# A gated mix of segment attention and a spectral filter on one core: the numerators of a segment loaded and normalised in two pieces instead of five, with rows dealt to chunks in another order and a new instruction plan

## The chip, the core and the metric

The kernel runs on one core of a Trainium2 chip. The metric is the device time of one execution in microseconds (us). Before the change the median of three runs is 243.28 us (242.96 to 243.37). The text calls the engines as the profile does: PE (TensorE's matmuls), PEld (its weight loads), DVE (VectorE), ACT (ScalarE), POOL (GpSimd) and SP (SyncE, which here only issues DMAs).

## The reference

Two branches read the same x of 2048 tokens by 640 features and are mixed token by token:

```python
g = sigmoid((x * gate_w).sum(-1, keepdims=True))
a = A(x)                       # 32 heads of 20, 4 segments of 512 tokens
b = irfft2(rfft2(x) * (w_r + 1j * w_i))
return g * a + (1 - g) * b

def A(x):                      # per head and segment s
    p = softmax(q @ k.T * scale + causal_mask)
    a_dot = p @ v
    a_mem = (phi(q) @ M) / (phi(q) @ z + 1e-6)     # memory of the earlier segments
    o = sigmoid(beta) * a_mem + (1 - sigmoid(beta)) * a_dot
    M, z = M + phi(k).T @ v, z + phi(k).sum(rows)
    return o @ wo              # o: the heads side by side, 640 columns
```

So 640 rows (32 heads times 20 elements) of attention output, each 512 tokens long per segment, must be divided by their head's denominator, joined by the memory's answer, and contracted with the 640 rows of wo.

## The kernel before

**The two branches.** The attention branch goes through the segments one by one: `project` makes q, k and v on PE, `qk_unit` makes the logits (in row tiles, four heads at once) with one exponential on ACT per unit and causal masks on DVE or POOL (`mask`, L1254 and L1255), `pv` multiplies by v. `mem_read_tile` asks the memory: matmuls into PSUM, then on DVE a sum (L1056), a reciprocal (L1059) and the product `mem_mul` (L1061 for segments 1 and 2, L1072 for segment 3), which writes the SBUF tile `mem`. The spectral branch (`fft`) is cut into small matmuls that fill PE between the attention units: for each of 16 frequency groups two products with the filter (`W_mul`, L1346, DVE) and two combinations (`W_add`, L1351, DVE or POOL). Its last step, `sum_Db` (L1388, DVE), makes the table `G`.

**Numerators.** `pv` leaves 512 tokens by 32 rows per head in PSUM (20 numerators, the denominator, padding); they are copied (`ub`) and stored in a DRAM scratch `u_scr`, head after head. When a segment's denominators have been inverted (`denominators`, a table `r4` with one row per head), `finish_tile` for its first quarter (a = 0) loads the 640 numerator rows back as the tile `oU`: a partition per head and part (32 heads times 4 = 128 partitions), five chunks of 512 tokens. Chunk c holds the elements 4c to 4c+3 of every head. One DMA (`ld_u`, L1412) and one multiplication by `r4` (`normal`, L1414, DVE or POOL) are made for each chunk. Segment 3 does the same for 24 heads with 5 parts and 4 chunks; its last 8 heads go another way. `mem_mul` writes its product in the same order of rows, so that after a store to `o_scr` and a transposing load (`mT`) it can be added to `oU` (`addmem`, L1427). Chunk c is then the stationary operand of the c-th `oproj` matmul of every output tile; `late_weights` loads the rows of wo in the order of the chunks (`wo` and, for segment 3, `wo3`).

**The order of the work.** Nothing is scheduled on the chip. `record` lists 2243 operations with what they read and write; `PLAN` is a list of as many integers, in the order in which the operations are emitted. The quotient by 16 is the operation's number, `v // 2 % 8` its engine and `v % 2` chooses a form for those matmuls that have two (`mode=-1`): whole array (one instruction of 128 columns of weights, L401) or four column tiles of 32 (L399). A second list gives each PSUM buffer its bank. `Sched.emit` puts the waits on semaphores. Every engine runs its own operations in that order, and one that waits holds up all behind it; SP issues nearly all DMAs in that order too. So PE's stream is a sequence of matmuls of three shapes: whole array, column tiles (`pv`, half of `v`, `Fb` always; others by choice) and row tiles (the logits, shown as 20*64 and 20*128).

Of the kernel before, what the change touches and what calls it, by code (L numbers as in the profile page):

```python
# [8 lines left out]
ALU = mybir.AluOpType  # L9
# [3 lines left out]
P = 128  # L13
S = 2048
D = 640
H = 32
DH = 20
NSEG = 4
L = 512
KD = 321  # L20
VW = 22
# [303 lines left out]
def dap(ap, off, *dims):  # L325
    return bass.AP(tensor=ap.tensor, offset=ap.offset + off, ap=[list(q) for q in dims])
# [24 lines left out]
class Kern:  # L351
# [65 lines left out]
    def dma(self, dst, src, nbytes, r, w, tr=False, name="", after=(), queues=("sp",)):  # L417
# [350 lines left out]
    def late_weights(self):  # L768
        b = self.b
# [722 lines left out]
```

## Time and profile before

| | |
|---|---|
| median of three runs | 243.28 us |
| the profiled execution: its time / its span | 241.93 us / 240.2 us |
| granted TensorE clock in it | 0.999 |
| largest group of instructions: ACT's exponentials, L1229 | 64 x 1878 ns = 120.2 us |
| DMA: moved, packets | 43.92 MB, 61897 |
| DMA issues of `oU<-u_scr` | 19 (15 of 128 KB, 4 of 120 KB) |

The span goes from the first instruction to the last; 1.7 us of the execution's time lie outside it. The page gives for each engine the time in which it ran an instruction, a row of 40 digits (tenths of each fortieth of the span), and the chain of work that ended last: from the last instruction back, at each step to what released it. Groups are shown as "out<-in" by the program's names with the count, the total and the mean in ns, and the idle time of the engine just before them. A window row gives the busy time of every engine in one stretch.

### The profile page before, as it was taken

The numbers are of one execution on the slowest core, as the hardware profiler recorded it, in microseconds if no ns is written. First come the engines' busy times: TensorE is split into PE (matmuls) and PEld (weight loads), VectorE is DVE, ScalarE is ACT, GpSimd is POOL, SyncE is SP. The second block draws the span as 40 slices with busy tenths as digits, with TensorE's granted clock in tenths as the row PEclk, the third lists the DMA queues.
The fourth block names the chain that finished last, engine by engine and source line by source line (L and its number), as shares of the span: only waits on it lengthen the run. The fifth ranks groups of instructions, "written<-read, shape, count | busy, mean of one in ns | idle before, by whom it ended". The sixth has DMA issues, their size and how long they took to land.

```text
span 240.2 us, 9491 instructions
## 1 busy us (share of the span) xinstructions
PE 220.6 (92%) x4004; PEld 138.0 (57%) x4018; DVE 209.2 (87%) x476; ACT 198.7 (83%) x226; POOL 134.2 (56%) x205
## 2 busy tenths in 40 slices
PE   6989979999999889999998999999978999799994
PEld 2865546665654547555755457656544555466673
DVE  0889979999999899999999989899999996867752
ACT  2489879999999988988999799997989598589321
POOL 8613154547647594676659563694686606753100
PEclk9999999999999999999999999999999999999999
DMA  7999979989959764269769847565875899594323
GB/s 196 317 242 271 235 221 154 296 217 166 233 153 206 177 179 142 68 185 176 236 183 200 182 113 232 167 184 178 200 174 167 177 214 120 114 191 129 109 104 113
DMA packets 61897, 43.92 MB, mean 183 GB/s; under 512 B 31232, under 2 KB 58656, under 8 KB 61856
## 3 DMA queue, kind: packets, MB, share of 16 engines
q1 hardware_dynamic: 60816, 42.76, 76.0%
q8 instruction: 31, 0.51, 0.9%
q10 hardware_dynamic: 1040, 0.57, 0.8%
q14 instruction: 10, 0.08, 0.1%
HBM read 23.42 MB, written 13.87 MB: 155 GB/s over the span
## 4 chain that ended last, share of the span: by engine, by line
PE 43%; DVE 32%; ACT 8%; POOL 6%; issue 5%; DMA 3%; SPq 2%; DVEq 0%; POOLq 0%
PE psum L401 39%; ACT ex L1229 5%; POOL exc L1255 4%; DVE Pt L1346 4%; PE psum L399 4%; DVE G L1388 3%; DVE ub L408 2%; DVE Yt L1351 2%; DMA x<-in_A_x_dram 2%; DVE va L408 2%; SPq L423 2%; DVE Ac L408 2%; DVE mem L1072 2%; ACT exc L1225 2%; DVE Bt L408 1%
## 5 line engine op out<-in xcount | busy, mean ns | idle before, releaser
L1229 ACT ACTIVATE ex<-psum 128x2048 bf16<-128x2048 f32 x64 | 120.2, 1878 | 12.8 <-PE psum L401 12.1
L1255 POOL TENSOR_SCALAR_AFFINE_SELECT ex<-ex 128x256 bf16<-128x256 bf16 (+2 forms) x93 | 54.5, 593 | 49.7 <-ACT ex L1229 34.9
L1255 POOL TENSOR_SCALAR_AFFINE_SELECT exc<-exc 128x512 bf16<-128x512 bf16 (+3 forms) x23 | 29.1, 1271 | 10.4 <-DVE exc L1254 7.3
L401 PE MATMUL psum<-qkp 20*64 20x64 bf16 (+5 forms) x1024 | 31.1, 266 | 3.4 <-DMA qkp<-qk_scr 1.3
L401 PE MATMUL psum<-xT,wk 128*128 128x256 bf16 (+1 forms) x276 | 29.7, 273 | 0.5 <-issue 0.5
L401 PE MATMUL psum<-xT,wq 128*32 128x256 bf16 (+1 forms) x161 | 25.1, 326 | 1.2 <-issue 1.0
L1346 DVE TENSOR_TENSOR Pt<-psum,Wt 128x642 bf16<-128x642 f32 x32 | 25.7, 821 | 0.3 <-PE psum L401 0.2
L401 PE MATMUL psum<-wv,xT 128*32 128x320 bf16 (+3 forms) x387 | 24.5, 300 | 0.4 <-DVE Pt L1346 0.4
L401 PEld LDWEIGHTS psum<-qkp 20*64 20x64 bf16 (+1 forms) x1024 | 12.6, 100 | 19.1 <-ACT ex L1229 8.6
L401 PEld LDWEIGHTS psum<-xT,wk 128*128 128x128 bf16 (+1 forms) x276 | 19.9, 97 | 5.2 <-issue 2.0
L401 PE MATMUL psum<-ex,va 128*32 128x384 bf16 (+2 forms) x384 | 20.4, 320 | 1.9 <-POOL ex L1255 0.7
L401 PE MATMUL psum<-wo,oU 128*128 128x320 bf16 (+1 forms) x114 | 18.6, 300 | 0.0
L836 POOL TENSOR_TENSOR xsb<-xf 128x320 bf16<-128x320 bf16 (+2 forms) x12 | 9.0, 750 | 16.7 <-DVE xsb L836 13.7
L401 PEld LDWEIGHTS psum<-wv,xT 128*32 128x32 bf16 (+1 forms) x387 | 13.8, 96 | 6.4 <-issue 1.1
L408 DVE CAST ub<-psum 128x512 bf16<-128x512 f32 x23 | 15.7, 683 | 1.9 <-PE psum L401 1.4
L408 ACT ACTIVATE ot<-psum 128x320 bf16<-128x320 f32 x21 | 8.7, 440 | 10.5 <-PE psum L399 4.2
L1225 ACT ACTIVATE exc<-psum 128x1024 bf16<-128x1024 f32 (+1 forms) x12 | 15.7, 1308 | 1.8 <-PE psum L401 1.4
L1388 DVE TENSOR_TENSOR G<-eo,psum 128x320 bf16<-128x320 f32 x32 | 14.9, 481 | 1.8 <-ACT eo L408 1.4
L401 PE MATMUL psum<-big,Ac 128*128 128x161 bf16 (+2 forms) x93 | 14.2, 258 | 0.7 <-DVE mem L1061 0.3
L1254 DVE TENSOR_TENSOR ex<-ex,mk 128x256 bf16<-128x256 bf16 (+2 forms) x35 | 13.7, 397 | 1.0 <-ACT ex L1229 0.9
L401 PEld LDWEIGHTS psum<-xT,wq 128*128 128x128 bf16 (+1 forms) x175 | 10.4, 97 | 7.2 <-issue 0.7
L401 PEld LDWEIGHTS psum<-ex,va 128*32 128x32 bf16 x384 | 8.0, 95 | 11.2 <-issue 2.7
(145 smaller groups left out, 459.5 us busy)
## 6 DMA issues: line engine op xcount, KB each, us to landing
qkp<-qk_scr SPq DMA_DIRECT2D x28, 160.0 KB
tt<-tab_tt SPq DMA_DIRECT2D x8, 512.0 KB, 4.2
u_scr<-ub SPq DMA_DIRECT2D x15, 256.0 KB, 3.9
qk_scr<-qu SPq DMA_DIRECT2D x12, 256.0 KB, 2.1
xsb<-in_A_x_dram SPq DMA_DIRECT2D x8, 320.0 KB, 4.9
oU<-u_scr SPq DMA_DIRECT2D x15, 128.0 KB, 2.6
out_dram<-ot SPq DMA_DIRECT2D x12, 160.0 KB
Wt<-in_B_w_r_dram SPq DMA_DIRECT2D x16, 80.2 KB, 4.1
```

The costliest lines, as they stand in the source:

```text
L399: h = e.matmul(dst, wt, r_, start=st, stop=sp_, **{**kw, "tile_position": (0, q), "skip_group_check": True})
L401: h = e.matmul(o_, l_, r_, start=st, stop=sp_, **({**kw, "skip_group_check": True} if mode < 0 else kw))
L408: fns = {"act": lambda e: e.activation(dst(), src(), ACT.Copy), "dve": lambda e: e.tensor_copy(dst(), src())}
L423: return e.dma_start(d_, s_)
L836: self.either(lambda e, dst=dst, src=src, d0=d0, n=n, op=op: e.tensor_tensor(xs.ap(o + dst, [D, 2], [1, n]), xf.ap(src + d0, [321, 2], [1, ...
L1072: self.one("dve", lambda e, q0=q0, n=n, d0=d0, dst=dst, src=src, bc=bc: e.tensor_tensor(self.mem.ap(o + d0, *dst), self.ps(bank, q0 * VW, ...
L1225: self.one("act", lambda e, i=i: e.activation(self.exc.ap(self.exco(s, g + i), [192, 4], [768, m], [1, 128]), self.ps(bank, 128 * i, [512, ...
L1229: self.one("act", lambda e: e.activation(self.ex.ap(*d), self.ps(bank, *q), ACT.Exp, scale=SC), n, [bank], [self.exb(s, 2 * pr + gp, ks + ...
L1254: fns = {"dve": lambda e: e.tensor_tensor(av(d0), av(s0), mk(), ALU.min), "pool": lambda e: e.affine_select(ap(d0), ap(s0), [[0, 4 * m], [ ...
L1255: "pool": lambda e: e.affine_select(ap(d0), ap(s0), [[0, 4 * m], [step, n // 64], [1, 64]], ALU.is_ge, 0.0, base=base, channel_multiplier=-1)}
L1346: self.one("dve", lambda e, ri=ri, Pt=Pt, Wt=Wt, wo_=wo_, bank=bank: e.tensor_tensor(Pt.ap(ri * 322, [644, 2], [1, KD]), self.ps(bank, 0, ...
L1388: self.one("dve", lambda e, q=q, n2=n2, bank=bank, eo=eo: e.tensor_tensor(self.G.ap(n2 * D + 639 * q, [1 - 2 * q, 320]), eo.ap(q, [1, 320] ...
```

## The change

It makes two loads and two multiplications of a segment's numerators where there were five (four for segment 3): chunks 0 to 2 in one and 3 to 4 in the other (0 to 1 and 2 to 3 for segment 3). For that the rows are dealt otherwise: part j of a head now holds elements 5j to 5j+4 (4j to 4j+3 in segment 3), one to each chunk, so that a partition's chunks lie next to each other in `u_scr` and one piece of a DMA is 3 KB or 2 KB instead of 1 KB. wo and wo3 are loaded in the same new order, with as many DMAs of the same size. `mem_mul` writes in the new order: it reads PSUM as before, element by element, but its writes were runs of 4 (5 in segment 3) neighbouring elements and are now single elements 128 elements apart. 22 operations fall away (11 DMAs and 11 multiplications).

The whole `PLAN` is new: 2221 entries, an order for every engine and new choices of engine, form and bank. Decoded with the numbers shifted by the removed operations:

| operations that change engine | moves |
|---|---|
| `W_add` | 13 from DVE to POOL, 6 back |
| masks of 128x256 | 14 to POOL, 5 to DVE |
| masks of 64x512 or 128x512 in `ex` | 11 to POOL, 9 to DVE |
| masks of 128x512 in `exc` | 5 to POOL, 1 to DVE |
| masks of 64x1024 in `exc` | 2 to DVE |
| `fold`, small | 2 to POOL, 8 to DVE; one large one to POOL |
| PSUM copies of 512 columns, ACT to DVE less DVE to ACT | 7-2 (`proj`), 6-3 (`pv`), 2-5 (`F1`), 1-3 (`Tb`), 1-1 |
| PSUM copies of 320 to 322 columns, likewise | 9-5 (`final`), 2-7 (`v`), 2-3 (`D`), 1-1 |
| first load of wk (240 KB) | from SP to ACT's queue |

`normal` becomes 8 instructions: `normal` of segment 0 on POOL (1536 and 1024 elements a partition), segment 1 on DVE (both), segment 2 one on each (1536 on DVE), segment 3 on DVE (1024 twice): in all 5 on DVE and 3 on POOL, before 11 and 8. The order of the exponentials on ACT and the amount of matmul work ahead of each stays nearly as it was. PE changes between its three shapes 211 times instead of 201.

```diff
     PLAN = ((
...
     def late_weights(self):
...
-            self.dma(lambda c=c: self.wo[c].ap(0, [1, D]), lambda c=c: dap(self.wo_d, 4 * c * D, [DH * D, H], [D, 4], [1, D]),
+            self.dma(lambda c=c: self.wo[c].ap(0, [1, D]), lambda c=c: dap(self.wo_d, c * D, [DH * D, H], [5 * D, 4], [1, D]),
...
-            self.dma(lambda c=c: self.wo3[c].ap(0, [1, D], np_=5 * nh), lambda c=c: dap(self.wo_d, 5 * c * D, [DH * D, nh], [D, 5], [1, D]),
+            self.dma(lambda c=c: self.wo3[c].ap(0, [1, D], np_=5 * nh), lambda c=c: dap(self.wo_d, c * D, [DH * D, nh], [4 * D, 5], [1, D]),
...
     def mem_read_tile(self, s, i):
...
-                self.mem.ap(i * D, [64, 2], [4, 16], [P, 5], [1, 4]), self.ps(bank, 0, [512, 2], [VW, 16], [4, 5], [1, 4]),
-                dn.ap(32, [16, 2], [1, 16], [0, 5], [0, 4]), ALU.mult), 640, [bank, rb], self.memb(s, i),
+                self.mem.ap(i * D, [64, 2], [4, 16], [1, 4], [P, 5]), self.ps(bank, 0, [512, 2], [VW, 16], [5, 4], [1, 5]),
+                dn.ap(32, [16, 2], [1, 16], [0, 4], [0, 5]), ALU.mult), 640, [bank, rb], self.memb(s, i),
...
-                (0, nh, 0, ([5 * nh, 2], [5, nh], [P, 4], [1, 5]), ([512, 2], [VW, nh], [5, 4], [1, 5]), ([0, DH],)),
+                (0, nh, 0, ([5 * nh, 2], [5, nh], [1, 5], [P, 4]), ([512, 2], [VW, nh], [4, 5], [1, 4]), ([0, DH],)),
...
     def finish_tile(self, s, a):
...
-            for c in range(nc_):
-                home = (self.after_mid(("oU", c)) if s == 0 else [b("phq", t) for t in range(5)] if s == 1 else
+            for c0, n in ((0, 3), (3, 2)) if s < 3 else ((0, 2), (2, 2)):
+                home = (self.after_mid(("oU", c0)) if s == 0 else [b("phq", t) for t in range(5)] if s == 1 else
                         [b("va", 0, lt) for lt in range(4)] if s == 2 else [b("wqa"), b("wqb")])
-                self.dma(lambda c=c: oT.ap(c * L, [1, L], np_=np_), lambda c=c: dap(self.ud.ap(), (s * 1024 + nd * c) * L, [32 * L, nh], [L, nd], [1, L]),
-                         np_ * L * 2, [b("ud", s, i) for i in range(ng)], [ob[c]], name="ld_u", after=home)
-                self.either(lambda e, c=c: e.tensor_tensor(oT.ap(c * L, [1, L], np_=np_), oT.ap(c * L, [1, L], np_=np_),
-                                                           self.r4[s].ap(0, [1, L], np_=np_), ALU.mult), L, [b("r4", s)], [ob[c]], name="normal")
+                self.dma(lambda c0=c0, n=n: oT.ap(c0 * L, [1, n * L], np_=np_),
+                         lambda c0=c0, n=n: dap(self.ud.ap(), (s * 1024 + c0) * L, [32 * L, nh], [nc_ * L, nd], [1, n * L]),
+                         np_ * L * 2 * n, [b("ud", s, i) for i in range(ng)], ob[c0:c0 + n], name="ld_u", after=home)
+                self.either(lambda e, c0=c0, n=n: e.tensor_tensor(
+                    oT.ap(c0 * L, [L, n], [1, L], np_=np_), oT.ap(c0 * L, [L, n], [1, L], np_=np_), self.r4[s].ap(0, [0, n], [1, L], np_=np_), ALU.mult),
+                    n * L, [b("r4", s)], ob[c0:c0 + n], name="normal")
```

233 rows, old and new, of the table PLAN are left out of this document.

## The prediction

> **What bounds the kernel now.** I read the page first, then windows of the span.
>
> ```profile
> span 240.2 us, 9491 instructions
> PE 220.6 (92%) x4004; PEld 138.0 (57%) x4018; DVE 209.2 (87%) x476; ACT 198.7 (83%) x226; POOL 134.2 (56%) x205
> PE 43%; DVE 32%; ACT 8%; POOL 6%; issue 5%; DMA 3%; SPq 2%; DVEq 0%; POOLq 0%
> ```
>
> The span lacks 1.7 us of the execution's 241.93 us; the median is 1.35 us above that execution, so I work out a difference and add it to 243.28. Three engines are over 80% busy, and the chain of work that ended last is shared by PE and DVE. No engine alone sets the time, so a stage must be looked at by itself:
>
> ```profile
> core 0: us, PE busy (x) PEld busy (x) DVE busy (x) ACT busy (x) POOL busy (x), PEclk, DMA share, GB/s
> 84.00:96.00 12.00, 10.98 (x183) 7.26 (x177) 11.92 (x26) 10.55 (x10) 8.52 (x13) 1.00 0.55 161
> 120.00:132.00 12.00, 11.04 (x215) 6.56 (x217) 11.80 (x26) 11.87 (x14) 8.55 (x14) 1.00 0.92 192
> 168.00:180.00 12.00, 10.10 (x192) 5.56 (x189) 11.26 (x30) 10.45 (x13) 9.26 (x16) 1.00 0.79 185
> 180.00:192.00 12.00, 10.57 (x199) 6.05 (x197) 11.68 (x29) 9.20 (x12) 7.34 (x9) 1.00 0.73 174
> 216.00:228.00 12.00, 12.00 (x228) 7.90 (x229) 8.92 (x27) 7.63 (x13) 3.70 (x6) 1.00 0.41 122
> ```
>
> The columns are window, its length, then busy time of each engine. In the first four stretches DVE is full and PE idles 1.0, 1.0, 1.9 and 1.4 us of 12: there DVE leads. At the end PE is full and DVE is not. So DVE work counts up to 192 us, PE work counts behind it, and what the change frees on DVE late is worth nothing. In 168 to 180 us the chain itself runs through the operation whose writes the change scatters:
>
> ```profile
> by line: DVE mem L1072 29.0%; DVE G L1388 19.1%; ACT ex L1229 15.6%; DVE dn L1059 11.4%; POOL ex L1255 5.5%; DVE ub L408 5.0%; DVE dn L1056 5.0%; DVE fbg L943 4.7%; issue 4.4%; DVE eo L408 3.4%; DVE va L408 3.3%; POOL gate L909 1.8%; DVE gg
> PEld psum L401 <- DVE mem L1072: 1.3, 3, 0.6
> ```
>
> The second row, of the waits in 168 to 192 us, says that PE waited 1.3 us for it: its matmuls need the PSUM banks that it reads.
>
> **The change part by part.** *Numerators.* Eleven multiplications on DVE and eight on POOL become five and three.
>
> ```profile
> L1414 DVE TENSOR_TENSOR oU<-oU,r 128x512 bf16<-128x512 bf16 x8 | 3.1, 413 | 0.0
> L1414 POOL TENSOR_TENSOR oU<-oU,r 128x512 bf16<-128x512 bf16 x7 | 8.0, 1155 | 1.1 <-DMA r<-r_scr 0.7 <-DMA oU<-u_scr 0.4
> L991 DVE TENSOR_TENSOR phq<-phq,qu 128x1024 bf16<-128x1024 bf16 x6 | 4.1, 683 | 0.1
> ```
>
> On DVE 512 elements take 413 ns and 1024 of the same kind 683, 0.53 ns an element; 1536 come to 953. Two of 1536 and three of 1024 are 3.96 us against 11 x 0.413 = 4.54: 0.6 saved. The repeated operand of the larger instruction (one row of `r4` for three chunks) isn't shown by itself; the masks repeat theirs over four heads and take 437 ns for 512, so I add nothing. On POOL some 1.5 us go, by 2.1 ns an element from this row and the 759 ns of 321 elements below.
>
> *Loads.* Nineteen become eight, and SP has eleven issues fewer:
>
> ```profile
> L423 SPq DMA_DIRECT2D oU<-u_scr x19: 516/602/1560, 165.8 to 221.1; - x19
> 178.18 6.08 SPq L423 DMA_DIRECT2D oU<-u_scr  x8
> ```
>
> That frees 11 x 0.6 = 6.6 us of SP; eight loads in a row hold it for 6.1 us, and the stores of `g_scr` and `r_scr` stand behind them. But SP's queue and DMA hold 2% and 3% of the chain. I take nothing and keep -1 us as an end. Each load now covers three chunks, so the first multiplication starts later by at most one issue; the output tiles that it feeds are filler for PE.
>
> *The scattered write of `mem_mul`.* Eight instructions of 640 elements (77 to 143 us) and four of 480 (172 to 180 us), same reads, writes now single 2-byte elements 256 bytes apart.
>
> ```profile
> L1061 DVE TENSOR_TENSOR mem<-psum,dn 128x640 bf16<-128x640 f32 x8 | 6.6, 825 | 0.4
> L1072 DVE TENSOR_TENSOR mem<-psum,dn 128x480 bf16<-128x480 f32 x4 | 2.8, 706 | 0.1
> L1280 DVE COPY Macc<-psum 128x154 f32<-128x154 f32 x4 | 1.2, 308 | 0.0
> L408 DVE COPY eo<-psum 128x321 f32<-128x321 f32 x4 | 1.9, 483 | 0.1
> L929 DVE COPY gT<-psum x4: 360/372/383, 75.9 to 180.3; 8x128 f32<-8x128 f32 x4
> ```
>
> The two copies with unbroken writes give 1.05 ns an element and 147 ns besides. By that line 640 elements take 818 ns: runs of four cost nothing now (825). 480 take 650: runs of five cost 56 ns. The last row (min/median/max) is a copy of 128 elements to single elements 32 bytes apart: 281 by the line, 372 measured, so 91 / 128 = 0.71 ns for each isolated write. The new write is not in the trace. It can't be quicker, since the same elements are read in the same sequence; the ends are 0 and 0.71 ns an element, and I take 0.71, the one row with isolated writes. Then 640 elements take 825 + 454 ns, 480 take 650 + 341: 8 x 0.45 = +3.6 us and 4 x 0.285 = +1.1 us on DVE.
>
> [...]
>
> *Work that changes its engine.* Counted from the new plan, with these prices:
>
> ```profile
> L1351 DVE TENSOR_TENSOR Yt<-Pt x18: 303/327/1464, 59.3 to 161.8; 128x321 bf16<-128x321 bf16 x18
> L1351 POOL TENSOR_TENSOR Yt<-Pt 128x321 bf16<-128x321 bf16 x14 | 10.6, 759 | 0.8 <-PE psum L401 0.8
> L1254 DVE TENSOR_TENSOR ex<-ex,mk 128x256 bf16<-128x256 bf16 x20 | 7.2, 368 | 0.1
> L1254 DVE TENSOR_TENSOR ex<-ex,mk 128x512 bf16<-128x512 bf16 x8 | 3.5, 437 | 0.0
> L1254 DVE TENSOR_TENSOR exc<-exc,mk 128x1024 bf16<-128x1024 bf16 x4 | 2.8, 690 | 0.7 <-POOL exc L1255 0.6
> L1255 POOL TENSOR_SCALAR_AFFINE_SELECT ex<-ex 128x256 bf16<-128x256 bf16 x44 | 21.0, 478 | 26.5 <-ACT ex L1229 19.8 <-DVE ex L1254 6.0
> L836 DVE TENSOR_TENSOR xsb<-xf 128x320 bf16<-128x320 bf16 x9 | 2.8, 326 | 0.7 <-POOL xsb L836 0.7
> L408 DVE CAST ub<-psum 128x512 bf16<-128x512 f32 x23 | 15.7, 683 | 1.9 <-PE psum L401 1.4 <-PE psum L399 0.4
> L408 DVE CAST ot<-psum 128x320 bf16<-128x320 f32 x11 | 5.3, 485 | 5.7 <-PE psum L399 3.0 <-PE psum L401 2.6
> ```
>
> From DVE to POOL go, net, seven `W_add` (7 x 0.33 = 2.3 us by the median), nine masks of 128x256 (9 x 0.37 = 3.3) and six of 512 elements (6 x 0.44 = 2.6); back come two masks of 1024 (1.4) and six small folds (2.0) less a large one and three small additions (0.5 + 3 x 0.2, at 0.53 ns an element and 0.14 us besides). PSUM copies between ACT and DVE: three of 512 columns more on DVE (2.0), two of 320 fewer (1.0), one of 256 more (0.4, by the line of the two copies). Sum for DVE: -2.3 - 3.3 - 2.6 + 1.4 + 2.0 - 1.1 + 1.4 = -4.5, with the multiplications -5.1 us. Means hold waits for POOL (the `W_add` row runs from 303 to 1464 ns), and POOL will be busier: I take -4. Nearly all of it is ahead of 168 us. POOL gains about 7 x 0.76 + 9 x 0.48 + masks of 512 less folds and multiplications, some +7 to +8 us on 134, half of it between 119 and 140 us. ACT has two copies fewer; PE's matmuls stay.
>
> *PE's order.* 211 changes of shape for 201, nine of the ten within 166 to 191 us. One costs about 0.10 us:
>
> ```profile
> 14.86 1.59 PE L401 MATMUL psum<-xT,wk 128*128 128x256 bf16 x13 [0.53 <-issue]
> 16.39 0.32 PE L401 MATMUL psum<-qkp 20*64 20x64 bf16 x24
> 49.38 1.04 PE L401 MATMUL psum<-xT,wk 128*128 128x256 bf16 x8
> 50.26 0.30 PE L401 MATMUL psum<-big,Ac 128*128 128x321 bf16 x1
> ```
>
> Eight matmuls of a shape, followed by the same shape, take 50.26 - 49.38 = 0.88 us, 0.11 each; thirteen before a change take 1.53, which is 0.10 more than 13 x 0.11. Ten are +1.0 us; in that stretch PE idles 3.3 us of 24, so half may be hidden: +0.5, ends 0 and 1.0.
>
> *Start.* wk's first load moves to ACT's queue; PE waited for x and then for wk at 6.4 and 7.1 us.
>
> ```profile
> GB/s 196 317 242 271 235 221 154 296 217 166 233 153 206 177 179 142 68 185 176 236 183 200 182 113 232 167 184 178 200 174 167 177 214 120 114 191 129 109 104 113
> ...
> 6.40 0.56 PEld L401 LDWEIGHTS psum<-id,x 128*128 128x128 bf16 x10 [0.57 <-DMA x<-in_A_x_dram]
> 7.13 0.10 PEld L401 LDWEIGHTS psum<-xT,wk 128*32 128x32 bf16 x4 [0.18 <-DMA wk<-in_A_wk_dram]
> ```
>
> It can gain the 0.18, or delay x by its 240 KB (1.2 us at the 196 GB/s of the first fortieth). I take 0, ends -0.2 and +1.2.
>
> *Sum.* Up to 168 us DVE gets -4 + 3.6 = -0.4, near nothing. From 168 to 192 us the four slower products stand on the chain: +1.1, and the changes of shape +0.5. Behind that PE's work is unchanged. -0.4 + 1.1 + 0.5 = +1.2, less 0.2 for ACT's two copies: **+1.0 us, 244.3 us.** Own range 243.8 to 246.0.
>
> **The rivals.** *DVE's relief shows (faster).* If an isolated write costs little, DVE is 4 to 5 us lighter in just the stretches where PE idles beside a full DVE (5.3 us in the four windows above). Half of it reaches the end, -2.1, with the shape changes -1.6: 241.7 us, from 239.5 to 242.6. It decides when the write costs under 0.3 ns an element (2.1 us in all). For it: the runs of four that cost nothing; against: the `gT` row. Chance 0.30.
>
> *POOL becomes the bound.* POOL's 8.55 of 12 us at 120 and 9.26 at 168 us grow by 1 to 2.5. A `W_add` there takes 0.43 us longer and stands in line behind masks; one piece of the numerators (1536 elements at 2.1 ns) holds POOL for 3.3 us. Seven `W_add` late by 0.43 are 3.0 us, most of it on the way to the next matmuls: +3 on +1, 246.5 (245.5 to 249). Against: POOL's waits are long now, so there is slack (26.5 us ahead of the one mask row). Chance 0.20.
>
> [...]
>
> *It does nothing measurable.* The exponentials keep their order, with PE's work ahead of each within 1 us, and the parts cancel: 243.3. Chance 0.11.
>
> *SP's freed issues count (faster).* Output tiles start earlier and fill PE's idle 1.4 us in 180 to 192: -1, 242.3. Chance 0.04.
>
> **How the numbers follow.** Forecast 0.35, rivals 0.30, 0.20, 0.11 and 0.04. A difference under 0.2% can't be told from none by a measurement of this kernel. Faster 0.30 + 0.04 = 0.34, same 0.11, slower 0.35 + 0.20 = 0.55. Range 240.0 to 247.5: the lowest tenth and the highest tenth of the two outer cases are left out.
>
> **What would show it.** `mem_mul` near 1.28 and 0.99 us if right, 0.82 and 0.65 if the write is free. DVE's busy time near 210 us, POOL's near 142. In 168 to 192 us DVE full, PE's idle above 3.3 us. Wrong if `mem_mul` stays short, or if PE's busy time or idle in 192 to 240 us moves by more than 1 us, which nothing here foresees.

## The result and the profile after

The changed kernel takes 271.74 us (median of four runs, 268.92 to 272.65) against 243.12 us (242.37 to 243.37) for the kernel before, run beside it: a ratio of 1.118 (95% interval 1.112 to 1.123), **28.6 us slower**. Here and in the table below a median is over all runs, while a ratio leaves out single executions that came out slow. The prediction had 244.3 us and a range up to 247.5. (From L429 on, lines of the changed kernel stand one lower than before: `mem_mul` is L1060 and L1071.)

The page of the changed kernel, its span, busy times, clock and chain:

```profile
span 270.2 us, 9488 instructions
PE 242.2 (90%) x4024; PEld 146.8 (54%) x4024; DVE 229.5 (85%) x456; ACT 198.9 (74%) x224; POOL 139.8 (52%) x216
PEclk9999999999997998999997757999955579999999
PE 57%; DVE 27%; DMA 6%; issue 3%; ACT 3%; POOL 2%; SPq 1%; DVEq 0%; ACTq 0%
```

ACT's busy time is as before, and POOL's 139.8 us are near the 142 that were foreseen. DVE has 20 us more, PE 22 us more although its products are the same, and the row of the granted clock, all nines before, has several dents. Next the groups of the changed kernel (count | total, mean in ns) and, from its waits, who stood behind the largest of them:

```profile
L1060 DVE TENSOR_TENSOR mem<-psum,dn 128x640 bf16<-128x640 f32 x8 | 24.0, 2995 | 0.3
L1071 DVE TENSOR_TENSOR mem<-psum,dn 128x480 bf16<-128x480 f32 x4 | 9.2, 2295 | 0.1
L1414 DVE TENSOR_TENSOR oU<-oU,r 128x1536 bf16<-128x1536 bf16 x2 | 1.9, 954 | 0.0
L1350 POOL TENSOR_TENSOR Yt<-Pt 128x321 bf16<-128x321 bf16 x21 | 15.4, 742 | 5.7 <-DVE Pt L1345 3.2 <-PE psum L401 2.4
```

```profile
PEld psum L401 <- DVE mem L1060: 13.8, 7, 2.7
PE psum L401 <- DVE mem L1060: 12.2, 7, 2.2
```

The product of 640 elements went from 825 to 2995 ns, that of 480 from 706 to 2295. Against unbroken writes (818 and 650 ns by the prediction's line) that is 2177 / 640 = 3.40 and 1645 / 480 = 3.43 ns for each isolated write, where the prediction took 0.71. In all 8 x 2.17 + 4 x 1.59 = 23.7 us more on DVE than before. PE waited for the eight products of segments 1 and 2 in seven places, 12.2 us in sum. The windows of the changed kernel show what followed:

```profile
core 0: us, PE busy (x) PEld busy (x) DVE busy (x) ACT busy (x) POOL busy (x), PEclk, DMA share, GB/s
84.00:96.00 12.00, 10.09 (x141) 5.27 (x140) 11.88 (x15) 9.10 (x9) 6.76 (x9) 0.88 0.92 182
120.00:132.00 12.00, 12.00 (x197) 7.69 (x196) 11.41 (x23) 11.92 (x11) 6.42 (x12) 1.00 0.83 204
144.00:156.00 12.00, 8.78 (x76) 4.14 (x77) 9.81 (x12) 4.79 (x4) 6.43 (x12) 0.68 0.18 49
192.00:204.00 12.00, 8.05 (x134) 4.06 (x135) 11.60 (x18) 7.22 (x8) 9.63 (x13) 0.67 0.56 156
204.00:216.00 12.00, 11.07 (x128) 4.24 (x125) 9.72 (x18) 6.54 (x6) 2.00 (x3) 0.50 0.49 139
```

Between the groups of products (120 to 132) all is well. Where the products stand (84 to 96, 144 to 156, 192 to 204), PE idles 2 to 4 us of 12, and the clock that it is granted falls to 0.88, 0.68 and 0.67. The last product ends at 205.5 us; in 204 to 216 PE is busy for 11.07 us, but at half the clock it gets through 128 matmuls; from 120 to 132 it was 197 (of other shapes in part).

### The profile page after: what moved, and what is told of

It is laid out like the page before. It is cut to its first block, busy times and chain, and to the rows that moved or that the text cites. A ratio compares the mean times of both kernels' runs of the same rounds, so it can differ in the third digit from the quotient of the medians.

```text
span 270.2 us, 9488 instructions
## 1 busy us (share of the span) xinstructions
PE 242.2 (90%) x4024; PEld 146.8 (54%) x4024; DVE 229.5 (85%) x456; ACT 198.9 (74%) x224; POOL 139.8 (52%) x216
## 4 chain that ended last, share of the span: by engine, by line
PE 57%; DVE 27%; DMA 6%; issue 3%; ACT 3%; POOL 2%; SPq 1%; DVEq 0%; ACTq 0%
PE psum L401 53%; DVE mem L1060 7%; DVE Pt L1345 5%; PE psum L399 4%; DVE mem L1071 4%; ACT ex L1228 2%; DMA u_scr<-ub 2%; DMA qk_scr<-qu 2%; DMA oU<-u_scr 1%; DVE dn L1058 1%; DVE ub L408 1%; DVE qu L408 1%; DMA x<-in_A_x_dram 1%; DVE Cp L408 1%; POOL Yt L1350 1%
## 5 line engine op out<-in xcount | busy, mean ns | idle before, releaser
L1254 POOL TENSOR_SCALAR_AFFINE_SELECT ex<-ex 128x256 bf16<-128x256 bf16 (+2 forms) x104 | 59.3, 579 | 69.0 <-ACT ex L1228 54.2
L401 PE MATMUL psum<-qkp 20*64 20x64 bf16 (+5 forms) x1024 | 32.8, 278 | 0.8 <-DMA qkp<-qk_scr 0.6
L401 PE MATMUL psum<-xT,wk 128*128 128x256 bf16 (+1 forms) x278 | 32.1, 283 | 0.1
L401 PE MATMUL psum<-xT,wq 128*128 128x512 bf16 (+1 forms) x173 | 31.1, 348 | 1.1 <-DVE mem L1060 1.0
L401 PE MATMUL psum<-wv,xT 128*32 128x320 bf16 (+3 forms) x400 | 27.9, 304 | 0.3 <-DVE Cp L408 0.3
L1060 DVE TENSOR_TENSOR mem<-psum,dn 128x640 bf16<-128x640 f32 x8 | 24.0, 2995 | 0.3
L408 DVE CAST ub<-psum 128x512 bf16<-128x512 f32 x26 | 17.6, 682 | 0.9 <-PE psum L401 0.4
L1350 POOL TENSOR_TENSOR Yt<-Pt 128x321 bf16<-128x321 bf16 x21 | 15.4, 742 | 5.7 <-DVE Pt L1345 3.2
L401 PE MATMUL psum<-big,Cp 128*128 128x321 bf16 (+1 forms) x71 | 17.5, 372 | 0.0
L408 DVE CAST qu<-psum 128x512 bf16<-128x512 f32 x21 | 14.6, 695 | 2.7 <-PE psum L401 2.5
```

The lines of the kernel that those rows point to most:

```text
L401: h = e.matmul(o_, l_, r_, start=st, stop=sp_, **({**kw, "skip_group_check": True} if mode < 0 else kw))
L408: fns = {"act": lambda e: e.activation(dst(), src(), ACT.Copy), "dve": lambda e: e.tensor_copy(dst(), src())}
L1060: self.one("dve", lambda e: e.tensor_tensor(self.mem.ap(i * D, [64, 2], [4, 16], [1, 4], [P, 5]), self.ps(bank, 0, [512, 2], [VW, 16], [5, ...
L1254: "pool": lambda e: e.affine_select(ap(d0), ap(s0), [[0, 4 * m], [step, n // 64], [1, 64]], ALU.is_ge, 0.0, base=base, channel_multiplier=-1)}
L1350: fn = lambda e, r=r, a0=a0, a1=a1, op=op, Pt=Pt, Yt=Yt: e.tensor_tensor(Yt.ap(r * 322, [1, KD]), Pt.ap(a0 * 322, [1, KD]), Pt.ap(a1 * 322 ...
```

## The experiments

Three theories stood against each other. **Theory 1**: the scattered write is dear, and it is DVE's time in these twelve products that the kernel loses. **Theory 2**: the new order of the engines is itself slower. **Theory 3**: the scattered writes hold up other engines at SBUF. As the experiments went on, others came from their results. Ratios are to the kernel before, run beside each; "half clock" is (1 - mean granted clock) / 0.5 times the span, since the clock in the records is 1.0 or 0.5 (in the changed kernel 0.50 from 196.2 to 219.9 us and 1.00 from 220.1 to 268.0), with a dash where the profiled execution is not comparable. Kernels of one group below (e0 to e2 and e5; e3a, e4, e6, e7; e8 to e10) ran on one chip; a difference across groups is that of the ratios, times 243.1 us.

| kernel | us, median | ratio (95%) | half clock, us |
|---|---|---|---|
| changed | 271.74 | 1.118 (1.112 to 1.123) | 47.6 |
| e1_runs_again | 238.18 | 0.984 (0.979 to 0.989) | 0 |
| e2_scatter_alone | 269.74 | 1.109 (1.103 to 1.116) | 30.9 |
| e3a_runs_12 | 247.97 | 1.021 (1.013 to 1.028) | - |
| e4_runs_in_pieces | 251.30 | 1.036 (1.029 to 1.042) | 13.9 |
| e5_by_halves | 238.88 | 0.986 (0.981 to 0.990) | 0 |
| e6_spread | 246.72 | 1.015 (1.007 to 1.023) | 3.9 |
| e7_five_again | 245.66 | 1.009 (1.004 to 1.014) | - |
| e8_equal_hold | 268.80 | 1.102 (1.096 to 1.107) | 41.2 |
| e9a_five_loads | 244.99 | 1.002 (0.997 to 1.008) | 13.7 |
| e9b_five_mults | 239.70 | 0.983 (0.979 to 0.987) | 0 |
| e10_one_scatter | 245.15 | 1.005 (1.000 to 1.010) | 13.7 |

### The price of a write, measured by itself (e0_probe)

```diff
+ run(v, lambda: cp(v, sb.ap(0, [128, 128]), ps([1, 128])))        # bf16, every 128th element
+ run(v, lambda: cp(v, sf.ap(0, [64, 128]), ps([1, 128])))         # float32, every 64th element
+ run(v, lambda: cp(v, sb.ap(0, [128, 64], [1, 2]), ps([2, 64], [1, 2])))
+ ...
```

> A kernel with nothing of the computation in it: x is copied to the output, and single instructions run one after the other with all other engines idle, three of each form: the product of mem_mul as it was and as it is (640 elements), the same into float32, copies of 128 elements with writes 1 to 128 elements apart, runs of 2 to 16, the same on 8 partitions, ACT and POOL. Theory 1 (the isolated write itself is dear on DVE): the old form takes 0.82 us and the new 2.9 to 3.0 us here too. Theory 3 (in the kernel other engines were in the way): the new form takes about 1.3 us when nothing else runs. What sets the price: if the width of the element, a bf16 copy at 32 bytes takes 0.28 + 128 x 3.4 ns less what is included = 0.55 to 0.75 us and a float32 copy at 256 bytes stays at 0.37; if the distance, both kinds take 0.37 us at 32 bytes and 0.55 to 0.75 at 256.

The groups of this kernel: the old form of the product, the new one, the new one into float32; then ACT and POOL with unbroken and with scattered writes of 128 elements; last the form of the `gT` row, copies of 128 elements on 8 partitions with writes 32 bytes apart, into bf16 and into float32:

```profile
L106 DVE TENSOR_TENSOR sb<-psum,dn 128x640 bf16<-128x640 f32 x3 | 2.5, 824 | 0.1
L107 DVE TENSOR_TENSOR sb<-psum,dn 128x640 bf16<-128x640 f32 x3 | 9.0, 2993 | 0.1
L108 DVE TENSOR_TENSOR sf<-psum,dn 128x640 f32<-128x640 f32 x3 | 3.7, 1238 | 0.1
L110 ACT ACTIVATE sb<-psum 128x128 bf16<-128x128 f32 x3 | 0.8, 278 | 96.7 <-DVE sb L109 96.6
L111 ACT ACTIVATE sb<-psum 128x128 bf16<-128x128 f32 x3 | 2.2, 740 | 0.1
L113 POOL COPY sb<-xs 128x128 bf16<-128x128 bf16 x3 | 0.9, 295 | 102.8 <-ACTq L74 102.7
L114 POOL COPY sb<-xs 128x128 bf16<-128x128 bf16 x3 | 2.3, 752 | 0.2
L66 DVE CAST sb<-psum 8x128 bf16<-8x128 f32 x3 | 2.0, 679 | 0.1
L66 DVE COPY sf<-psum 8x128 f32<-8x128 f32 x3 | 1.1, 374 | 0.1
```

The windows of DVE's copies of 128 elements, three in each row (busy time / 3 is one copy). In order: bf16 with writes 2, 4, 8, 16 and 256 bytes apart; float32 with writes 4, 16 and 256 bytes apart; bf16 in runs of two, 256 bytes apart:

```profile
core 0: us, DVE busy (x) ACT busy (x) POOL busy (x), PEclk, DMA share, GB/s
47.95:48.94 0.99, 0.87 (x3) 0.00 (x0) 0.00 (x0) 1.00 0.00 0
48.94:49.95 1.01, 0.91 (x3) 0.00 (x0) 0.00 (x0) 1.00 0.00 0
49.95:51.38 1.43, 1.33 (x3) 0.00 (x0) 0.00 (x0) 1.00 0.00 0
51.38:53.65 2.27, 2.17 (x3) 0.00 (x0) 0.00 (x0) 1.00 0.00 0
60.35:62.64 2.29, 2.18 (x3) 0.00 (x0) 0.00 (x0) 1.00 0.00 0
62.64:63.62 0.97, 0.87 (x3) 0.00 (x0) 0.00 (x0) 1.00 0.00 0
64.59:65.84 1.25, 1.15 (x3) 0.00 (x0) 0.00 (x0) 1.00 0.00 0
69.54:70.76 1.22, 1.11 (x3) 0.00 (x0) 0.00 (x0) 1.00 0.00 0
70.76:71.73 0.97, 0.88 (x3) 0.00 (x0) 0.00 (x0) 1.00 0.00 0
```

With all other engines idle the new product takes 2993 ns, as in the kernel: nothing was in its way there. The price hangs on the **width of the element**. An isolated 4-byte write costs (1.11 - 0.87) / 3 / 128 = 0.63 to 0.73 ns, at 16 as at 256 bytes: that is the 0.71 of the `gT` row, whose own form takes 374 ns here (372 in the kernel) and 679 ns when nothing but the element becomes 2 bytes wide. An isolated 2-byte write costs (2.18 - 0.87) / 3 / 128 = 3.4 ns, at 16 as at 256 bytes. Two 2-byte elements side by side cost nothing at 256 bytes (0.88 against 0.87). It isn't DVE alone: the same 128 single elements cost ACT 462 ns and POOL 457 ns, 3.6 ns each.

The product into float32, whose writes are single 4-byte elements 512 bytes apart, takes 1238 ns: (1238 - 818) / 640 = 0.66 ns an element above the unbroken line, in step with the float32 copies.

### The write taken back, and the write alone (e1_runs_again, e2_scatter_alone)

```diff
-                self.mem.ap(i * D, [64, 2], [4, 16], [1, 4], [P, 5]), self.ps(bank, 0, [512, 2], [VW, 16], [5, 4], [1, 5]),
+                self.mem.ap(i * D, [64, 2], [4, 16], [P, 5], [1, 4]), self.ps(bank, 0, [512, 2], [VW, 16], [4, 5], [1, 4]),
```

(and the like for segment 3; e2 makes the opposite edit in the kernel before.)

> The changed kernel with the old order of writes in mem_mul (runs of 4 and 5 elements), all else as changed; the memory's rows then stand in the old order beside numerators in the new. Theory 1 (the scattered write is the whole loss): mem_mul back at 0.82 and 0.71 us, DVE's busy time near 206 us, the granted clock back at 1.0 and the time 239 to 245 us. Theory 2 (the new order of the engines is itself slower): above 250 us with mem_mul at 0.82 us.

> The kernel before with nothing changed but the order of mem_mul's writes (single elements 256 bytes apart), so that the memory's rows stand in another order than the numerators'. Theory 1: mem_mul at 3.0 and 2.3 us, 8 x 2.17 + 4 x 1.6 = 23.8 us more on DVE, which is full there: 243.1 + 22 to 29 = 265 to 272 us, with a lower granted clock. Theory 2: at most 255 us.

The page of e1_runs_again:

```profile
span 236.4 us, 9488 instructions
PE 223.9 (95%) x4024; PEld 140.2 (59%) x4024; DVE 206.0 (87%) x456; ACT 197.2 (83%) x224; POOL 140.0 (59%) x216
PE 57%; DVE 16%; ACT 13%; DMA 7%; issue 3%; SPq 1%; POOL 1%; DVEq 0%
```

Theory 1 holds in both directions: without the scatter the changed kernel takes 238.2 us, the scatter alone makes 269.7 us of the kernel before. Theory 2 falls. All else in the change is worth **-4.0 us** (-1.6%, from -1.1 to -2.1%): PE is now 95% of the span and DVE's share of the chain is 16%, half of what it was before.

### Is it the time, or the writes? (e4_runs_in_pieces, e8_equal_hold)

```diff
+            self.one("dve", lambda e: [e.tensor_tensor(
+                self.mem.ap(i * D + 64 * q + 4 * h, [P, 5], [1, m]), self.ps(bank, 512 * q + VW * h, [4, 5], [1, m]),
+                dn.ap(32 + 16 * q + h, [0, 5], [0, m]), ALU.mult) for h in range(16) for q in range(2) for m in (4,)][-1], 640,
```

(e8; in e4 one piece for each h, of both q.)

> The changed kernel with the old runs of 4 and 5 elements in mem_mul, but each product cut into 16 (12) instructions of 40 elements, so that it holds DVE and the PSUM bank for as long as the scattered product did: 16 x (147 + 42) ns = 3.0 us and 12 x 189 = 2.3 us. The memory's rows stand in the old order. Theory 1 (DVE's time alone): within 2 us of the changed kernel, 268 to 274 us, with a mean granted clock of 0.90 to 0.95. Theory 3 (the scattered writes also hold up other engines at SBUF): under 265 us.

> The kernel with the products in pieces held DVE for 1.79 and 1.37 us only, since instructions of 40 elements follow each other every 112 ns. Here the pieces have 20 elements: 32 x (112 - 20 x 1.05 = 91) ns = 2.9 us and 24 x 91 = 2.2 us, the hold of the scattered product, with writes in runs of 4 and 5. The memory's rows stand in the old order. Theory 1 (DVE's time alone, whatever it writes): 264 to 273 us and half clock for 30 us or more. Theory 3 (scattered writes hold up others at SBUF): at most 260 us.

e4 missed its aim: the pieces overlap, and sixteen held DVE for 1.79 us, not 3.0. So 251.3 us is the answer to about 10 us of delay (8 x 0.97 + 4 x 0.66), and neither theory's number applies. e8 has the right length, in DVE's timeline:

```profile
80.21 2.81 DVE L1060 TENSOR_TENSOR mem<-psum,dn 128x20 bf16<-128x20 f32 x32
84.88 2.83 DVE L1060 TENSOR_TENSOR mem<-psum,dn 128x20 bf16<-128x20 f32 x32
```

With harmless writes and nearly the same hold it takes 268.8 us. Theory 3 falls: DVE's time, and PE's wait for the bank, are enough for all but 3.9 us of the changed kernel's time by the ratios, and the twelve holds of e8 are 2.0 us shorter in sum (2.82 and 2.15 us each).

### More than the time: 23.7 us became 33 (e6_spread, e3a_runs_12, e10_one_scatter)

From e1 to the changed kernel are (1.118 - 0.984) x 243.1 = 33 us, nine more than DVE was given.

```diff
-                (0, nh, 0, ([5 * nh, 2], [5, nh], [1, 5], [P, 4]), ([512, 2], [VW, nh], [4, 5], [1, 4]), ([0, DH],)),
+                (0, nh, 0, ([5 * nh, 2], [5, nh], [1, 5], [P, 4]) if i == 2 else ([5 * nh, 2], [5, nh], [P, 4], [1, 5]), ...
```

(e10; e3a has the edit of e1 in segments 1 and 2 alone. e6 has all runs back, three copies for each copy of numerators on DVE, and four instructions for each `W_mul`:)

```diff
-                    Pt.ap(ri * 322, [644, 2], [1, KD]), self.ps(bank, 0, [0, 2], [1, KD]), Wt.ap(wo_, [644, 2], [1, KD]), ALU.mult), 2 * KD,
+                    Pt.ap(ri * 322 + c, [644, 2], [1, n]), self.ps(bank, c, [0, 2], [1, n]), Wt.ap(wo_ + c, [644, 2], [1, n]), ALU.mult)
+                    for c, n in ((0, 80), (80, 80), (160, 80), (240, 81))][-1], 2 * KD,
```

> The changed kernel with the old runs in mem_mul (0.82 us), and about as much more DVE time as the scatter cost put elsewhere in small portions: each of the 32 W_mul cut in four (+3 x 0.147 us each, 14.1 us) and each copy of numerators on DVE cut in three (26 x 0.294 = 7.6 us), 21.7 us in all against 23.8. Theory 4 (twelve long holds of PE bring the granted clock down, and that is what lies beyond the 23.8 us): clock at 0.99 or more and 250 to 260 us. Theory 1a (every us on DVE counts alike, however it is dealt out): 238 + 0.91 x 33.5 = 266 to 272 us, with the clock down as before.

> The changed kernel with the old runs in segments 1 and 2 (eight products) and the scattered write in segment 3 (four products, +1.6 us each). If the loss goes by DVE's time: 238.2 + 33.5 x 6.4 / 23.8 = 247 us (245 to 249). If the falling clock needs many stalls: 238.2 + 6.4 at most = 241 to 244.6, clock 0.99 or more.

> The changed kernel with the old runs in eleven of the twelve products and the scattered write in one alone, the third of segment 3 (+1.6 us on DVE near 178 us); the memory's rows in the old order but there. If a single wait of PE of about 2 us is enough to halve the granted clock for some us: half clock in the trace for 3.4 to 13.7 us after it and 241 to 245.5 us. If the clock needs many waits: no half clock before the end and 238 to 240 us.

e6 fell short too: its DVE is only 7.2 us busier than e1 (213.2 against 206.0), not 21.7. These 7.2 us cost 7.5, with 3.9 us of half clock, so it separates little. e3a came out near the 247 us of proportion to DVE's time, but e10 shows that this was chance: **one** of those four products, 1.6 us more on DVE, makes about 5.1 of their 9.0 us ((1.005 - 0.984) and (1.021 - 0.984) x 243.1; the intervals leave either some 2 us of play). Windows of e5_by_halves, which has no scatter, and of e10 (columns as above):

```profile
180.00:192.00 12.00, 11.16 (x218) 6.06 (x210) 11.28 (x24) 8.56 (x12) 6.52 (x8) 1.00 0.94 188
```

```profile
168.00:180.00 12.00, 9.38 (x217) 5.24 (x209) 11.28 (x28) 11.05 (x11) 10.03 (x13) 0.98 0.82 227
180.00:192.00 12.00, 11.68 (x123) 4.66 (x124) 9.33 (x19) 5.96 (x8) 3.68 (x8) 0.50 0.67 173
192.00:204.00 12.00, 11.86 (x202) 6.46 (x201) 9.91 (x19) 8.20 (x9) 6.79 (x7) 0.95 0.45 117
```

One wait, and for 13.7 us the clock is halved: from 180 to 192 us PE gets through 123 matmuls where e5 has 218. The same place, PE's wait ahead of two matmuls of `fcat,omh`, in the timelines of e9b_five_mults (told below) and of e10:

```profile
179.09 0.30 PE L401 MATMUL psum<-fcat,omh 128*66 128x128 bf16 x2 [1.28 <-POOL omh L921]
```

```profile
180.32 0.40 PE L401 MATMUL psum<-fcat,omh 128*66 128x128 bf16 x2 [1.92 <-POOL ex L1254]
```

In e9b the wait of 1.28 us left the clock at 1.0 (mean 1.000); in e10 the one of 1.92 went with half the clock. But by the windows of e10 (0.98 of the clock from 168 to 180 us, which is 0.4 to 0.6 us at half) the clock fell at about 179.5 us, when 1.0 to 1.2 us of that wait had gone by, so 1.28 us isn't shown to be a safe length. (The wait in e10 is put down to POOL; the product, and the smaller one behind it, left the bank at 180.18 us, 0.14 us before PE went on.)

What a microsecond of half clock costs is an estimate, by e10 against e9b on the same chip: the span is 243.9 against 238.7 us, 0.6 of it the longer wait, the other 4.6 us over 13.7: 0.33. At that price the 47.6 us of the changed kernel cost 16 of its 33 us, which leaves about 17 for DVE's 23.7 us directly. The pages of the changed kernel and of e1, which have the same list of work, agree: PE is busy 18.3 us longer (242.2 against 223.9), as its matmuls are slower at half the clock (one of `big,Cp`, 128x321 whole array, took 469 ns on the mean from 204 to 216 us, at 0.50, and 308 from 220 to 268, at 1.00), and idle 15.5 us longer (28.0 against 12.5 us of the span).

### The loads (e7_five_again, e9a_five_loads, e9b_five_mults) and a faster version (e5_by_halves)

```diff
-                self.dma(lambda c0=c0, n=n: oT.ap(c0 * L, [1, n * L], np_=np_),
+                self.dma(lambda c0=c0, n=n: [oT.ap(c * L, [1, L], np_=np_) for c in range(c0, c0 + n)],
...
-                self.either(lambda e, c0=c0, n=n: e.tensor_tensor(
-                    oT.ap(c0 * L, [L, n], [1, L], np_=np_), oT.ap(c0 * L, [L, n], [1, L], np_=np_), self.r4[s].ap(0, [0, n], [1, L], np_=np_), ALU.mult),
+                self.either(lambda e, c0=c0, n=n: [e.tensor_tensor(
+                    oT.ap(c * L, [1, L], np_=np_), oT.ap(c * L, [1, L], np_=np_), self.r4[s].ap(0, [1, L], np_=np_), ALU.mult)
+                    for c in range(c0, c0 + n)][-1], n * L, [b("r4", s)], ob[c0:c0 + n], name="normal")
```

(e9a has the first edit alone, e9b the second; all stand on e5, whose product is two instructions in the order of their writes:)

```diff
+            self.one("dve", lambda e: [e.tensor_tensor(
+                self.mem.ap(i * D + 64 * q, [P, 5], [4, 16], [1, 4]), self.ps(bank, 512 * q, [1, 5], [VW, 16], [5, 4]),
+                dn.ap(32 + 16 * q, [0, 5], [1, 16], [0, 4]), ALU.mult) for q in range(2)][-1], 640, [bank, rb], self.memb(s, i),
```

> The changed kernel, whole computation, with mem_mul's writes in runs of 64 and 60 elements: two instructions of 320 (240) elements, one for each PSUM bank, that read PSUM at every fifth (fourth) element. By the line of the unbroken copies two of 320 take 0.97 us against 0.82: theory 1 gives the time of the kernel with the old runs plus 0 to 1.8 us, 240 to 246. If reading PSUM at a distance of 20 bytes costs as much as writing at a distance, the pair takes 2.5 to 3 us and the time stays above 262.

> The whole computation, by halves as before (238.9 us), with the numerators again in five loads and five multiplications of one chunk each at the same places in the order (four in segment 3). The prediction's prices: loads nothing (1 us at most), DVE 12 x 0.413 against 3.96 us = +1.0 us: 238.5 to 241. Rival (the two larger loads are what makes the new kernel faster than the old): 242 to 244 us.

> The whole computation, by halves (238.9 us), with five loads of the numerators but the two larger multiplications. Theory 5 (with five loads the numerators land later, POOL's multiplication waits for them and omh, for which PE waits, stands behind it): 243 to 247 us with a wait of PE for omh near 178 us, as with loads and multiplications both in five. Theory 6 (the five multiplications were the loss): within 1 us of 238.9.

> The whole computation, by halves, with the two larger loads but five multiplications (four in segment 3). The prediction's prices: 0.6 to 1.0 us more on DVE, 238.9 to 240. Theory 5: likewise. Theory 6 (the five multiplications were the loss): 243 to 247 us.

**e5 computes the whole change and is faster than both kernels**: 238.9 us, 1.4% under the kernel before (1.0 to 1.9%). Its pair takes 2 x 484 ns; reading PSUM at every fifth element costs nothing that shows (484 ns for 320 elements, 483 by the unbroken line), writing at single elements did.

e7 fell outside both expectations, 5.7 us above e5 by the ratios, and e9a and e9b part it: five multiplications cost nothing that can be told (239.7 us; 0.983 against 0.986), five loads 4.6 us more than they by the ratios, on the same chip (the intervals leave some 2 us of play). Theory 5 holds in outline, but what lands late is another load. POOL's timeline in e5, then the chain of e9a:

```profile
172.07 5.19 POOL L1420 TENSOR_TENSOR oU<-oU,r 128x1536 bf16<-128x1536 bf16 x2 [0.62 <-DMA r<-r_scr]
177.20 0.22 POOL L921 TENSOR_TENSOR omh<-gg,omh 128x8 bf16<-128x8 f32 x1
```

```profile
170.72 3.40 DMA r<-r_scr
174.25 5.17 POOL oU L1426 x2
179.42 0.17 POOL omh L927
```

With SP's extra issues ahead of it the load of `r4` (`r<-r_scr`) goes from 168.08 to 170.72 us. POOL's multiplication of numerators waits for it, starts at 174.25 us instead of 172.07 (in e9b at 173.27), ends 2.2 us later, and `omh`, for which PE waits, stands behind it on POOL. PE's wait at the place shown above, here in the timelines of e5 and of e9a, grows with it, and in this execution the clock is halved for 13.7 us as in e10:

```profile
177.62 0.27 PE L401 MATMUL psum<-fcat,omh 128*66 128x128 bf16 x2 [0.45 <-DVE mem L1076]
```

```profile
179.64 0.42 PE L401 MATMUL psum<-fcat,omh 128*66 128x128 bf16 x2 [1.75 <-POOL omh L927]
```

By its windows (0.96 of the clock from 168 to 180 us, 0.8 to 1.1 us at half) the clock fell at about 179.0 us, when 1.0 to 1.3 us of the wait had gone by. It isn't so in every execution of e9a: one had a mean clock of 0.993 and took 242.53 us, where the one shown had 0.972 and took 245.73. The five multiplications of e9b make POOL's piece longer too, but only to a wait of 1.28 us, and the clock stays at 1.000.

## Why the prediction was wrong

- **The step that failed: the price in "The scattered write of `mem_mul`".** Instruction, place, counts and direction were right; the price was 3.4 ns an element, not 0.71, so the term was +23.7 us and not +4.7. The 0.71 came from the one row with isolated writes, and was made an end of the range as well. That row (`gT`) writes 4-byte elements, `mem` has 2-byte ones; the probe has the row's own form with 2-byte elements, and there it is dear as well (679 ns for 374), so nothing else set the row apart. An upper end from a row of another element type was no end.
- **The other terms came out in sum, in part by luck.** Without the write they come to -4 + 0.5 - 0.2 = -3.7 us; e1 measured -4.0 (about -5.2 to -2.8). DVE's relief was 3.2 us (209.2 to 206.0) where 4 were taken; 1536 elements took 954 ns where 953 were worked out; POOL came to 140 where 142 were foreseen. Taking 4 of the 5.1 us counted rests on reading long `W_add` times as waits for POOL. In the trace of before the five `W_add` on DVE that ran while POOL was idle took 0.32 to 0.33 us, and those of 0.86, 1.38 and 1.46 us ran beside instructions of POOL; but eight more beside POOL took 0.30 to 0.40, so what makes one wait isn't shown. That the relief up to 168 us reaches the end isn't shown: with five loads in this order (e9a, 1.002) nothing of the 4 us is left, though DVE's work is that of e5. So the loads, put at nothing, are worth about as much as the whole sum.
- **"DVE work counts up to 192 us" was too little, and not quite the way.** With the right price the sum is -3.7 + 23.7 = +20.0, 263 us, some 8 us short. Against e1 PE idles only 15.5 us longer, not 23.7; the other 18.3 us are its matmuls at the lower clock. That clock was 0.999 before, and the prediction treated it as given; in the changed kernel its five stretches at 0.50 (83.5 to 86.9, 100.6 to 104.0, 144.9 to 151.8, 155.2 to 165.4 and 196.1 to 220.0 us) began in a wait of PE for a product, of 1.6 to 2.2 us, or up to 1.7 us behind its end, and e1, with the short products, kept 1.000.
- **"I take nothing and keep -1 us" for SP's freed issues was wrong in this order of work**: they are worth about 4.6 us (e9a against e9b), since with them one wait of PE is 0.45 us (e5) or 1.28 (e9b), with no half clock, and without them 1.75 (e9a), with 13.7 us of it in the profiled execution. The rival that counted them (-1 us) had the sign and not the mechanism. An order of the engines made for five loads wasn't tried; the kernel before has one and takes 243.
- **POOL as the bound** didn't come about: e1 has POOL at 140 us and is faster. But the rival's mechanism, a piece of numerators on POOL that holds up what stands behind it, is what bites in e9a. Its time was also added up wrongly: +3 on +1 is 247.3 us, not 246.5.
- A row was misread: the 1.3 us in 168 to 192 us are waits of PEld, the weight loads. PE itself waited 0.8 us there for `mem_mul` (0.5 and 0.3). The forecast took no term from it.
- Not settled: the new changes of shape and the first load of wk, which no run takes apart. PE is busy 223.9 us in e1, 3.3 more than before at full clock, of which the shapes were to explain 1.0.

## What to carry to other kernels

When an edit changes the order of writes, ask how many bytes lie side by side (here an isolated write of two bytes cost 3.4 ns, one of four about 0.7): a row with other element types prices another instruction, and a range that rests on it must reach further. Loops over the same elements can be turned so that writes run on and reads jump; here that kept the whole change and removed the cost. And a delay of an engine that feeds PE isn't worth its length alone: look for the places where PE already waits, since 1.6 us more on DVE cost about 5 at one of them.

## What the runs showed of the hardware that was not expected

- In e0_probe an isolated 2-byte write into SBUF cost 3.4 ns on DVE and 3.6 on ACT and POOL, an isolated 4-byte write on DVE 0.63 to 0.73 ns, two neighbouring 2-byte elements nothing (0.88 us for three copies against 0.87). In e5 reading PSUM at every fifth float32 showed no price (484 ns for 320 elements, 483 by the unbroken line).
- Single waits of PE of 1.75 us (e9a) and 1.92 us (e10) each went with 13.7 us at half the granted clock. A wait of 1.28 us (e9b) did not, nor did one of 1.66 us at 206 us in the kernel before. In the changed kernel one of 1.92 us that ended at 82.0 us was followed by 0.50 from 83.6 to 86.8 us, while one of 1.75 us that ended at 94.8 us left the clock at 1.00 up to 100.5 us: length alone doesn't decide. From 180 to 192 us in e10 PE shows 11.68 of 12 us busy while the clock stays at 0.50.
- In e4 the pieces of a product overlapped on DVE: sixteen of 40 elements, 190 ns each, held it for 1.79 us, 112 ns a piece, where 3.0 us had been worked out.
